# Row-tiled transposes, another order of the value products, and a selection product for the router's logits in a linear-attention kernel

## The chip, the cores and the metric

One core of a Trainium2 chip runs the whole program. The metric is the device time of one execution in microseconds (us). TensorE (PE; its weight loads are PEld), VectorE (DVE), ScalarE (ACT) and GpSimd (POOL) each run their own instructions in order and wait for each other by semaphores; SyncE (SP) issues most DMAs.

## The reference

Gated linear attention, then two expert layers. Only the attention is touched by the change.

```python
def _attn_ref(q, k, v, f_logit):        # B, H, S, D = 4, 8, 768, 48
    f = 1.0 / (1.0 + np.exp(-f_logit))
    for t in range(S):
        state = f[:, :, t, :, None] * state + np.einsum('bhd,bhe->bhde', k[:, :, t], v[:, :, t])
        y[:, :, t] = np.einsum('bhd,bhde->bhe', q[:, :, t], state)
# _moe_ref:  logits = x @ w_gate (3072 x 8); tokens go to 8 experts of 384 places each
#            in the order of their logits; relu(x @ w1[e]) @ w2[e]
# _moe2_ref: rms norm, then (silu(xn @ w_gate) * (xn @ w_val)) @ w_out
```

## The kernel before

The attention works on 16 units, each a batch and a pair of heads. Head 0 of a pair lies on partitions 0 to 47, head 1 on partitions 64 to 111; the 768 positions run along the free axis in six chunks of 128. In each chunk the keys are scaled by a scan of the decays (`W`, giving `kt`) and the queries by another (`P`, giving `qt`), so that a chunk is a masked product of `kt` and `qt` (`at`) times `v`, plus the state at the chunk's start (`st`) times `qt`.

The loop at the end of `attention` is a pipeline written out by hand. In turn `i` TensorE's queue holds, in this order: `values(i - 2)` (the outputs `yp`, from 10 products with `st` and 12 with `at`), `logits_turn` in three of the turns, `k_back(i)` (five chunks of `kt` transposed into `kn`), `inner(i)` (12 products into four banks, three chunks and one head to a bank), `sums(i)` (10 products into `U`), and `logits` in the turns in which a batch is complete. The router's logits of a batch leave `logits` as `lgT`, 4 pairs of heads with 32 rows each; the four are added up later: `logits_turn` transposes three blocks of 128 tokens into a bank, and `logits_sum` on VectorE reduces over the pairs into `lg`. The last batch goes through the same functions behind the loop's last values, and the routing starts on its `lg`.

VectorE's queue in turn `i` holds `scans(i + 1)` (scan `P`, reciprocal, scan `W`, then `logits_sum` if one is due, then `kt`) and then the scan `st` behind `sums(i)`. ScalarE copies out of PSUM: `YT` from `yp`, `kn`, `at`, `lgT`. GpSimd makes `qt` and masks `at`.

PSUM has eight banks: four in the pool behind `bank()`, taken in rotation by `k_back`, `inner`, `logits` and `logits_turn`, two for `yp`, one for `U`, and one for `one`, a column of ones that every scan reads as its second operand.

TensorE's instructions address a part of its array. `k_back` and `logits_turn` use all of it (128 rows, 128 columns), `inner` the two halves of the rows (64 by 128), `sums` and the products with `at` the two halves of the columns (128 by 64), the products with `st` quarters (64 by 64). One fp32 product of two heads stands in the trace as two passes for each head; a transpose is one pass.

Of the kernel before, what the change touches and what calls it, by code (L numbers as in the profile page):

```python
# [7 lines left out]
F32 = mybir.dt.float32  # L8
# [5 lines left out]
OP = mybir.AluOpType  # L14
AX = mybir.AxisListType
# [65 lines left out]
class Route:  # L81
# [27 lines left out]
    def range(self, n):  # L109

        nc, v = self.tc.nc, self.v
        m = self.m0[:, 0:n]
        nc.vector.tensor_reduce(out=m, in_=self.lg[:, 0:n], axis=AX.X, op=OP.max)
        nc.vector.tensor_reduce(out=v[:, 1:2], in_=self.lg[:, 0:n].rearrange("p n e -> p (n e)"), axis=AX.X, op=OP.min)
        nc.vector.tensor_reduce(out=v[:, 0:1], in_=m, axis=AX.X, op=OP.max)
        nc.vector.tensor_reduce(out=v[:, 2:3], in_=m, axis=AX.X, op=OP.min)
        nc.vector.tensor_scalar(v[:, 1:3], v[:, 1:3], -1.0, None, op0=OP.mult)
        self.n = n
# [149 lines left out]
def spin(nc, o, ident, n):  # L268

    for _ in range(n):  # L270
        nc.tensor.matmul(o, ident, ident, start=True, stop=True)
# [52 lines left out]
def attention(tc, fT, kT, qT, vL, YT, w_gate, lg, pmin, ident, gcol, rms_g, extra):  # L324
# [4 lines left out]
    nc = tc.nc  # L329
    NU, _, S = fT.shape  # L330
    B, H, D = 4, 8, 48
    C = 128
    NP = H // 2
    NC = S // C
    ctx = ExitStack()
    pool = lambda name, bufs, **kw: ctx.enter_context(tc.tile_pool(name=name, bufs=bufs, **kw))
    cst = pool("a_cst", 1)
    wk = pool("a_wk", 2)
    ps = pool("a_ps", 4, space=PSUM)
    psl = pool("a_psl", 1, space=PSUM)  # L340
# [7 lines left out]
    def raw(nm, i):  # L348
        return RAW[nm, i % NR]

    def load(names, i):
        if not 0 <= i < NU:
            return
        for nm in names:
            if nm == "v":
                nc.sync.dma_start(V[i % NV].rearrange("p n h d -> p (n h d)"), vL[i])
                continue
            src, t = dict(f=fT, k=kT, q=qT)[nm][i], raw(nm, i)
            if i < NR:
                nc.sync.dma_start(t, src)  # L360
                continue
            for h in range(2):
                nc.sync.dma_start(t[64 * h:64 * h + D], src[64 * h:64 * h + D])

    HF = (slice(0, S // 2), slice(S // 2, S))
    for t in HF:
# [5 lines left out]
    nc.gpsimd.memset(mask, 1.0)  # L372
    nc.gpsimd.affine_select(out=mask, in_=mask, pattern=[[1, C]], compare_op=OP.is_ge, fill=0.0, base=0,
                            channel_multiplier=-1)
    one = psl.tile([128, 1], F32, name="one")
    nc.vector.memset(one, 1.0)
    one = one[:, 0:1].to_broadcast([128, S])
    wgp = cst.tile([128, NP, 32], F32, name="wgp")
    nc.vector.memset(wgp, 0.0)
    YP = [psl.tile([128, 384], F32, name=f"yp{i}") for i in range(2)]  # L380
# [9 lines left out]
    def bank():  # L390
        return ps.tile([128, 384], F32, name="bank")

    G, FS, P, W, KT, QT, KN, AT, ST, LG, EZ = ({} for _ in range(11))

    def decays(i):
        if not 0 <= i < NU:
            return
        G[i] = wk.tile([128, S + 1], F32, name="G")
        FS[i] = wk.tile([128, NC], F32, name="fs")
        for t in HF if i == 0 else (slice(0, S),):  # L400
            nc.scalar.activation(G[i][:, t], raw("f", i)[:, t], AF.Sigmoid)
        nc.scalar.activation(FS[i], raw("f", i)[:, 0:S:C], AF.Sigmoid)
# [18 lines left out]
    def scans(i):  # L421
        g = G[i]
        P[i] = wk.tile([128, S], F32, name="P")
        W[i] = wk.tile([128, S], F32, name="W")
        nc.vector.memset(g[:, 0:S:C], BIG * 1.0e8)
        nc.vector.tensor_tensor_scan(out=P[i], data0=g[:, :S], data1=one, initial=1.0, op0=OP.mult, op1=OP.min)
        ends = P[i][:, C - 1:S:C]
        nc.vector.reciprocal(g[:, C:S + 1:C], ends)
        nc.vector.tensor_tensor_scan(out=W[i][:, ::-1], data0=g[:, S:0:-1], data1=one, initial=1.0, op0=OP.mult,
                                     op1=OP.max)  # L430
        while turned:
            logits_sum(*turned.pop(0))
        QT[i] = wk.tile([128, S], F32, name="qt", bufs=3)
        for g in range(2):
            t = slice(g * 384, g * 384 + 384)
            nc.gpsimd.tensor_tensor(out=QT[i][:, t], in0=raw("q", i)[:, t], in1=P[i][:, t], op=OP.mult)
        EZ[i] = wk.tile([128, NC - 1], F32, name="e")
        nc.gpsimd.tensor_tensor(out=EZ[i], in0=ends[:, 0:NC - 1], in1=FS[i][:, 1:], op=OP.mult)
        KT[i] = wk.tile([128, S], F32, name="kt")
        nc.vector.tensor_tensor(out=KT[i], in0=raw("k", i), in1=W[i], op=OP.mult)  # L440

    def ends(i):
        if on(i):
            nc.scalar.copy(pall[:, i], P[i][:, C - 1:S:C])
            nc.scalar.copy(Z[i % 2][:, :, 1:], EZ[i][:, None, :].to_broadcast([128, D, NC - 1]))

    def k_back(i, gs=(0, 1)):
        if 0 in gs:
            KN[i] = wk.tile([128, NC, 128], F32, name="kn")
        for g in gs:  # L450
            m = 3 - g
            o = bank().rearrange("p (n c) -> p n c", n=3)
            for n in range(m):
                c0 = (3 * g + n) * C
                nc.tensor.transpose(o[:, n, :], KT[i][:, c0:c0 + C], ident)
            nc.scalar.copy(KN[i][:, 3 * g:3 * g + m], o[:, 0:m])

    def inner(i, gs=(0, 1)):

# [29 lines left out]
    def values(i):  # L489

        b, p = units[i]
        yp = YL if i == NU - 1 else YP
        todo = [(h, n, True) for h, n in ((0, 1), (1, 3), (0, 2), (1, 4), (1, 5), (1, 1), (0, 3), (1, 2), (0, 4), (0, 5))]
        todo += [(h, n, False) for n in range(NC) for h in range(2)]
        first, last = {}, {}
        for m, (h, n, _) in enumerate(todo):
            first.setdefault((h, n // 3), m)
            last[h, n // 3] = m
        for m, (h, n, state) in enumerate(todo):
            d, c = slice(64 * h, 64 * h + D), slice(n * C, (n + 1) * C)  # L500
            nc.tensor.matmul(yp[n // 3][d, (n % 3) * C:(n % 3 + 1) * C],
                             ST[i][d, :, n] if state else V[i % NV][:, n, h, :],
                             QT[i][d, c] if state else AT[i][:, h, n, :],
                             start=m == first[h, n // 3], stop=m == last[h, n // 3])
        for g in range(2):
            cp = nc.vector.tensor_copy if g and i == NU - 1 else nc.scalar.copy
            cp(YT[0:112, b, p, 384 * g:384 * g + 384], yp[g][0:112])
# [8 lines left out]
        nc.scalar.copy(LG[b, g], o)  # L516

    def logits_turn(b, g):
        o = bank()
        for n in range(3):  # L520
            nc.tensor.transpose(o[:, n * 128:n * 128 + 128], LG[b, g][:, n * 128:n * 128 + 128], ident)
        turned.append((b, g, o))

    def logits_sum(b, g, o):
        nc.vector.tensor_reduce(out=lg[:, NC * b + 3 * g:NC * b + 3 * g + 3, :],
                                in_=o.rearrange("p (n a e) -> p n e a", n=3, a=NP)[:, :, 0:8], axis=AX.X, op=OP.add)

    YL = []
    on = lambda i: 0 <= i < NU
    turned = []  # L530
    o = bank()[:, 0:128]
# [10 lines left out]
    for i in range(-1, NU + 2):  # L542
        if i - 1 in extra:
            extra[i - 1](bank()[:, 0:256])
        if on(i - 2):
            values(i - 2)
        if on(i - 3) and units[i - 3][1] == NP - 1:
            for g in range(2):
                logits_turn(units[i - 3][0], g)
        load("v", i + 2 if i > -1 else NU)  # L550
        if i < 0:
            decays(1)
        if i > 0 and on(i):
            k_back(i)
        if i == NU - 1:
            extra["range"]()
        if i < 0:
            for t in HF:
                scans_half(t)
            for g in range(2):  # L560
                k_back(0, (g,))
                inner(0, (g,))
            ends(0)
        elif on(i + 1):
            scans(i + 1)
        if on(i):
            if i:
                inner(i)
            decays(i + 2)
            sums(i)  # L570
            if i == 0:
                spin(nc, bank()[:, 0:128], ident, 11)
            ends(i + 1)
        if on(i - 2) and units[i - 2][1] == NP - 1:
            for g in range(2):
                logits(units[i - 2][0], g)
            if i == NU + 1:
                for g in range(2):
                    logits_turn(units[i - 2][0], g)
                    logits_sum(*turned.pop(0))  # L580
        if i == NU - 1:
            extra["edges"](bank())
        load("fkq", i + 4)
        if i == NU - 1:
            for _ in range(2):
                YL.append(bank())
                nc.vector.memset(YL[-1][32:64], 0.0)
        if i == NU:
            nc.vector.tensor_reduce(out=pmin, in_=pall.rearrange("p a b -> p (a b)"), axis=AX.X, op=OP.min)
# [664 lines left out]
```

## Time and profile before

| | us |
|---|---|
| median of 3 runs (lowest, highest) | 832.44 (831.95, 832.62) |
| the profiled execution's own time | 832.29 |
| its span, first to last instruction | 830.6 |
| busy in the span: PE, PEld | 805.3, 777.4 |
| busy in the span: DVE, ACT, POOL | 485.7, 391.3, 274.0 |

The attention ends at about 116 us of the span, the routing follows until about 150 us, and the rest is the two expert layers, in which TensorE is hardly ever idle. Busy times of matmuls are modelled at their ends, and matmuls overlap: what a block of TensorE work costs is best read from its start to the start of the next block.

### The profile page before, as it was taken

The numbers are of one execution on the slowest core, as the hardware profiler recorded it, in microseconds if no ns is written. First come the engines' busy times: TensorE is split into PE (matmuls) and PEld (weight loads), VectorE is DVE, ScalarE is ACT, GpSimd is POOL, SyncE is SP. The second block draws the span as 40 slices with busy tenths as digits, with TensorE's granted clock in tenths as the row PEclk, the third lists the DMA queues.
The fourth block names the chain that finished last, engine by engine and source line by source line (L and its number), as shares of the span: only waits on it lengthen the run. The fifth ranks groups of instructions, "written<-read, shape, count | busy, mean of one in ns | idle before, by whom it ended". The sixth has DMA issues, their size and how long they took to land.

```text
span 830.6 us, 16688 instructions
## 1 busy us (share of the span) xinstructions
PE 805.3 (97%) x6641; PEld 777.4 (94%) x6641; DVE 485.7 (58%) x875; ACT 391.3 (47%) x834; POOL 274.0 (33%) x327
## 2 busy tenths in 40 slices
PE   8999996999999999999999999999999999999996
PEld 7888875899999999999999999999999999999996
DVE  8988868579888988575444434334343434334332
ACT  5777644256645555476343343424343443434221
POOL 7877600367777777250202010110102010110100
PEclk9999997899999999999999999999999999999999
DMA  9997227586887788341000000000000000000000
GB/s 270 224 219 193 58 92 290 184 298 226 284 280 245 248 282 301 127 152 39 10 12 20 1 20 2 20 1 20 4 17 20 1 21 1 20 1 21 1 20 20
DMA packets 43829, 88.56 MB, mean 107 GB/s; under 512 B 5440, under 2 KB 23104, under 8 KB 43744
## 3 DMA queue, kind: packets, MB, share of 16 engines
q1 hardware_dynamic: 34672, 70.89, 27.6%
q0 software_dynamic: 3072, 9.44, 3.4%
q10 hardware_dynamic: 6000, 7.09, 2.4%
q8 instruction: 54, 0.88, 0.5%
q14 instruction: 31, 0.25, 0.1%
HBM read 70.89 MB, written 16.52 MB: 105 GB/s over the span
## 4 chain that ended last, share of the span: by engine, by line
PE 61%; issue 9%; DVE 8%; ACT 2%; DMA 1%; POOL 1%; ACTq 0%; DVEq 0%; POOLq 0%
PE o L624 5%; PE o L622 5%; PE o L623 5%; PE g L622 5%; PE g L624 5%; PE g L623 5%; PE v L624 5%; PE v L623 5%; PE v L622 5%; PE x L623 3%; PE x L624 2%; PE x L622 2%; DVE nb L1006 2%; DVE w L813 2%; PE h L623 2%
## 5 line engine op out<-in xcount | busy, mean ns | idle before, releaser
L1178 DVE TENSOR_TENSOR hf<-sg,v 128x256 f32<-128x256 f32 x144 | 60.0, 417 | 165.1 <-PE v L624 114.9
L944 POOL TENSOR_TENSOR xlo<-xn,xhi 128x256 fp32r<-128x256 f32 x36 | 29.5, 823 | 311.9 <-ACT xhi L943 311.9
L1181 ACT CAST hh<-hf 128x256 fp32r<-128x256 f32 x144 | 58.6, 407 | 132.9 <-DVE hf L1178 132.9
L624 PE MATMUL g<-xhi,w 128*128 128x256 f32 x432 | 119.3, 276 | 0.0
L623 PE MATMUL g<-xlo,w 128*128 128x256 f32 x432 | 119.3, 276 | 0.0
L624 PE MATMUL v<-xhi,w 128*128 128x256 f32 x432 | 119.2, 276 | 0.0
L622 PE MATMUL v<-xhi,w 128*128 128x256 f32 x432 | 119.2, 276 | 0.0
L623 PE MATMUL v<-xlo,w 128*128 128x256 f32 x432 | 119.2, 276 | 0.0
L622 PE MATMUL g<-xhi,w 128*128 128x256 f32 x432 | 119.2, 276 | 0.0
L1182 DVE TENSOR_TENSOR hl<-hf,hh 128x256 fp32r<-128x256 f32 x144 | 61.3, 426 | 68.1 <-ACT hh L1181 67.6
L624 PE MATMUL o<-w,hl 128*128 128x384 f32 x288 | 98.6, 342 | 0.0
L622 PE MATMUL o<-w,hh 128*128 128x384 f32 x288 | 97.5, 339 | 0.2 <-ACT hh L1181 0.2
L623 PE MATMUL o<-w,hh 128*128 128x384 f32 x288 | 97.1, 337 | 0.0
L1176 ACT ACTIVATE sg<-g 128x256 f32<-128x256 f32 x144 | 55.3, 384 | 87.8 <-PE g L624 87.3
L622 PEld LDWEIGHTS g<-xhi,w 128*128 128x128 f32 x432 | 81.1, 188 | 0.0
L624 PEld LDWEIGHTS g<-xhi,w 128*128 128x128 f32 x432 | 81.1, 188 | 0.0
L622 PEld LDWEIGHTS v<-xhi,w 128*128 128x128 f32 x432 | 81.1, 188 | 0.0
L624 PEld LDWEIGHTS v<-xhi,w 128*128 128x128 f32 x432 | 81.1, 188 | 0.0
L623 PEld LDWEIGHTS v<-xlo,w 128*128 128x128 f32 x432 | 81.1, 188 | 0.0
L623 PEld LDWEIGHTS g<-xlo,w 128*128 128x128 f32 x432 | 81.0, 188 | 0.0
L1009 POOL TENSOR_TENSOR nr<-nr,ne 128x384 f32<-128x384 f32 x36 | 61.6, 1711 | 42.8 <-ACT hh L1082 11.8
L623 PE MATMUL x<-hl,w 128*128 128x384 f32 x192 | 65.7, 342 | 3.5 <-DVE hl L1083 3.5
(237 smaller groups left out, 1893.8 us busy)
## 6 DMA issues: line engine op xcount, KB each, us to landing
wraw<-in_moe_w_dram SPq DMA_DIRECT2D x32, 768.0 KB, 7.8
v<-in_v_rows_dram SPq DMA_DIRECT2D x16, 288.0 KB, 5.1
x_dram<-xrows SPq DMA_DIRECT2D x24, 192.0 KB, 5.4
nraw<-in_moe_w_gate_dram SPq DMA_DIRECT2D x12, 384.0 KB, 4.9
nraw<-in_moe_w_val_dram SPq DMA_DIRECT2D x12, 384.0 KB, 4.4
nraw<-in_moe_w_out_dram SPq DMA_DIRECT2D x12, 384.0 KB, 4.3
raw_f<-in_f_logit_turned_dram SPq DMA_DIRECT2D x26, 144.0 KB, 5.4
raw_k<-in_k_turned_dram SPq DMA_DIRECT2D x26, 144.0 KB, 4.6
```

What stands on the lines that cost most here:

```text
L622: nc.tensor.matmul(out, lhs[0], rhs[0], start=first, stop=False)
L623: nc.tensor.matmul(out, lhs[0], rhs[1], start=False, stop=False)
L624: nc.tensor.matmul(out, lhs[1], rhs[0], start=False, stop=last)
L813: eng.tensor_tensor(out=lo, in0=raw, in1=hi.bitcast(F32), op=OP.subtract)
L944: eng.tensor_tensor(out=lo, in0=s, in1=hi.bitcast(F32), op=OP.subtract)
L1006: nc.vector.scalar_tensor_tensor(out=b, in0=hw, scalar=-0x40000000, in1=b, op0=OP.bitwise_and, op1=OP.bitwise_or)
L1009: nc.gpsimd.tensor_tensor(out=r, in0=r, in1=e2.bitcast(F32), op=OP.mult)
L1176: nc.scalar.activation(sg, pg, AF.Silu)
L1178: nc.vector.tensor_tensor(out=h, in0=sg, in1=pv, op=OP.mult)
L1181: nc.scalar.copy(hh, h)
L1182: nc.vector.tensor_tensor(out=hl, in0=h, in1=hh.bitcast(F32), op=OP.subtract)
```

## The change

Three things are rewritten. `k_back` transposes each chunk head by head, 48 rows at a time, all chunks of a head into one bank of its own, and copies each bank with one instruction. `values` issues the 12 products with `at` ahead of the 10 with `st`. `logits_turn` replaces each transpose by a product with a constant matrix `sel` (128 by 8, four stacked unit matrices), which adds up the pairs; its outputs go to 192 columns of a bank that also holds `one`, and `logits_sum` is one copy for a batch instead of two reductions.

```diff
-    one = psl.tile([128, 1], F32, name="one")
+    bank0 = psl.tile([128, 512], F32, name="bank0")
+    one = bank0[:, 0:1]
     nc.vector.memset(one, 1.0)
-    one = one[:, 0:1].to_broadcast([128, S])
+    one = one.to_broadcast([128, S])
+    lgp = bank0[:, 64:64 + lg.shape[1] * 8].rearrange("p (n e) -> p n e", e=8)
+    sel = cst.tile([128, 8], F32, name="sel")
+    nc.vector.tensor_reduce(out=sel, in_=ident.rearrange("q (p e) -> q e p", p=NP)[:, 0:8, :], axis=AX.X, op=OP.add)
...
     def k_back(i, gs=(0, 1)):
         if 0 in gs:
             KN[i] = wk.tile([128, NC, 128], F32, name="kn")
-        for g in gs:
-            m = 3 - g
-            o = bank().rearrange("p (n c) -> p n c", n=3)
-            for n in range(m):
-                c0 = (3 * g + n) * C
-                nc.tensor.transpose(o[:, n, :], KT[i][:, c0:c0 + C], ident)
-            nc.scalar.copy(KN[i][:, 3 * g:3 * g + m], o[:, 0:m])
+        a, m = (0, NC - 1) if len(gs) == 2 else (3 * gs[0], 3 - gs[0])
+        o = [bank()[:, 0:m * D].rearrange("p (n d) -> p n d", n=m) for _ in range(2)]
+        for n in range(m):
+            for h in range(2):
+                d = slice(64 * h, 64 * h + D)
+                nc.tensor.transpose(o[h][:, n, :], KT[i][d, (a + n) * C:(a + n + 1) * C], ident[d, d])
+        for h in range(2):
+            nc.scalar.copy(KN[i][:, a:a + m, 64 * h:64 * h + D], o[h])
...
     def values(i):
-        todo = [(h, n, True) for h, n in ((0, 1), (1, 3), (0, 2), (1, 4), (1, 5), (1, 1), (0, 3), (1, 2), (0, 4), (0, 5))]
-        todo += [(h, n, False) for n in range(NC) for h in range(2)]
+        todo = [(h, n, False) for n in range(NC) for h in range(2)]
+        todo += [(h, n, True) for h, n in ((0, 1), (1, 3), (0, 2), (1, 4), (1, 5), (1, 1), (0, 3), (1, 2), (0, 4), (0, 5))]
...
     def logits_turn(b, g):
-        o = bank()
         for n in range(3):
-            nc.tensor.transpose(o[:, n * 128:n * 128 + 128], LG[b, g][:, n * 128:n * 128 + 128], ident)
-        turned.append((b, g, o))
-
-    def logits_sum(b, g, o):
-        nc.vector.tensor_reduce(out=lg[:, NC * b + 3 * g:NC * b + 3 * g + 3, :],
-                                in_=o.rearrange("p (n a e) -> p n e a", n=3, a=NP)[:, :, 0:8], axis=AX.X, op=OP.add)
+            nc.tensor.matmul(lgp[:, NC * b + 3 * g + n, :], LG[b, g][:, n * 128:n * 128 + 128], sel, start=True, stop=True)
+        if g:
+            turned.append(slice(NC * b, NC * b + NC))
+
+    def logits_sum(t):
+        nc.vector.tensor_copy(lg[:, t], lgp[:, t])
```

TensorE's queue from the `sums` of the turn in which the first batch is complete to the `sums` of the next turn, before, with the output tile, the moving and the stationary operand and the shape of the output (L501 is `values`, L513 `logits`, L521 `logits_turn`):

```order
L482 MATMUL U<-v_113,kn 48x48 x10
L513 MATMUL bank<-YT,wgp 32x384 x8
L501 MATMUL yp_129<-qt,st 48x128
...
L501 MATMUL yp_130<-qt,st 48x128 x2
L501 MATMUL yp_129<-at,v_112 48x128 x6
L501 MATMUL yp_130<-at,v_112 48x128 x6
L521 MATMUL bank<-ident,lgT 128x128 x6
L455 MATMUL bank<-ident,kt 128x128 x5
L468 MATMUL bank<-qt,kt 128x128 x12
L482 MATMUL U<-v_114,kn 48x48 x10
```

The same place now:

```order
L487 MATMUL U<-v_113,kn 48x48 x10
L518 MATMUL bank<-YT,wgp 32x384 x8
L506 MATMUL yp_131<-at,v_112 48x128 x6
L506 MATMUL yp_132<-at,v_112 48x128 x6
L506 MATMUL yp_131<-qt,st 48x128
...
L506 MATMUL yp_132<-qt,st 48x128 x2
L525 MATMUL bank_125<-sel,lgT 128x8 x6
L459 MATMUL bank<-ident,kt 128x48 x10
L473 MATMUL bank<-qt,kt 128x128 x12
L487 MATMUL U<-v_114,kn 48x48 x10
```

The products with `at` moved ahead of those with `st`; in a turn without logits (no L513, no L521) they now follow `sums` of the turn before directly; `k_back` has ten transposes of 48 columns for five of 128; the six products with `sel` stand where six transposes (L521) stood.

VectorE's queue in that turn, with the semaphores each waits for, before:

```order
L426 SCALAR_TENSOR_TENSOR P<-G,one 128x768 [waits DVE_49,Pool_49]
L428 RECIPROCAL G<-P 128x6 [waits DVE_49]
L429 SCALAR_TENSOR_TENSOR W<-G,one 128x768 [waits DVE_49]
L525 TENSOR_REDUCE lg<-bank 128x24 [waits PE_49] x2
L440 TENSOR_TENSOR kt<-raw_k_107,W 128x768 [waits DMAHW6_49,DMAHW5_49,DVE_49]
```

And now:

```order
L430 SCALAR_TENSOR_TENSOR P<-G,bank_125 128x768 [waits DVE_49,PE_49,Pool_49]
L432 RECIPROCAL G<-P 128x6 [waits DVE_49]
L433 SCALAR_TENSOR_TENSOR W<-G,bank_125 128x768 [waits DVE_49]
L530 COPY lg<-bank_125 128x48
L444 TENSOR_TENSOR kt<-raw_k_107,W 128x768 [waits DMAHW6_49,DMAHW5_49,DVE_49]
```

The scan `P` of the next unit, which reads `one`, now waits for TensorE, that is for the products with `sel` into the same bank; the reductions' wait behind `W` is gone. In the other turns the scans' waits are as before.

## Rows read from the trace of the kernel before

**Rows 1.** The page, first part: busy us (share of the span) and instructions

```profile
PE 805.3 (97%) x6641; PEld 777.4 (94%) x6641; DVE 485.7 (58%) x875; ACT 391.3 (47%) x834; POOL 274.0 (33%) x327
```

**Rows 2.** Busy time by stretch: length, PE PEld DVE ACT POOL, granted clock, DMA

```profile
47.28:53.66 6.38, 5.69 (x95) 4.97 (x94) 4.54 (x7) 4.08 (x11) 3.30 (x7) 1.00 1.02 228
53.66:59.35 5.69, 5.69 (x95) 5.01 (x94) 5.43 (x7) 4.56 (x12) 4.73 (x7) 1.00 1.03 221
...
72.87:78.50 5.63, 5.63 (x95) 4.95 (x93) 3.63 (x7) 4.08 (x11) 2.40 (x6) 1.00 0.78 210
```

**Rows 3.** Timeline of VectorE: two neighbouring scans `P` (start, length)

```profile
27.75 1.75 DVE L426 TENSOR_TENSOR_SCAN P<-G,one 128x768 f32<-128x768 f32 x1
...
33.36 1.75 DVE L426 TENSOR_TENSOR_SCAN P<-G,one 128x768 f32<-128x768 f32 x1
```

**Rows 4.** Timeline of TensorE over one turn with logits and the next

```profile
65.04 0.77 PE L455 MATMUL bank<-ident,kt 128*128 128x128 f32 x5
65.73 1.68 PE L468 MATMUL bank<-qt,kt 48*128 48x128 f32 x24
67.35 0.66 PE L482 MATMUL U<-v,kn 128*48 128x48 f32 x20
67.93 1.50 PE L513 MATMUL bank<-YT,wgp 112*32 112x384 f32 x16
69.36 1.42 PE L501 MATMUL yp<-qt,st 48*48 48x128 f32 x20
70.71 1.52 PE L501 MATMUL yp<-at,v 128*48 128x128 f32 x24
72.16 0.88 PE L521 MATMUL bank<-ident,lgT 128*128 128x128 f32 x6
72.87 0.71 PE L455 MATMUL bank<-ident,kt 128*128 128x128 f32 x5
73.51 0.38 PE L468 MATMUL bank<-qt,kt 48*128 48x128 f32 x2
```

**Rows 5.** Timeline of ScalarE around 65 us

```profile
64.50 0.48 ACT L507 COPY YT<-yp 112x384 f32<-112x384 f32 x1 [0.64 <-PE yp L501]
65.16 0.48 ACT L507 COPY YT<-yp 112x384 f32<-112x384 f32 x1 [0.18 <-PE yp L501]
65.68 0.75 ACT L456 COPY kn<-bank 128x384 f32<-128x384 f32 x2
```

**Rows 6.** Timeline of weight loads: two neighbouring ones of fp32 products, of transposes

```profile
119.26 0.19 PEld L195 LDWEIGHTS T<-far,ident 128*128 128x128 f32 x1
...
119.37 0.19 PEld L195 LDWEIGHTS T<-far,ident 128*128 128x128 f32 x1
...
72.16 0.14 PEld L521 LDWEIGHTS bank<-ident,lgT 128*128 128x128 f32 x1 [0.18 <-ACT YT L507]
...
72.21 0.14 PEld L521 LDWEIGHTS bank<-ident,lgT 128*128 128x128 f32 x1
```

**Rows 7.** Timeline of TensorE in the first turn with transposed logits

```profile
48.67 0.34 PE L468 MATMUL bank<-qt,kt 48*128 48x128 f32 x1 [0.69 <-POOL e L438]
```

**Rows 8.** Timeline of VectorE in that turn

```profile
44.61 1.75 DVE L426 TENSOR_TENSOR_SCAN P<-G,one 128x768 f32<-128x768 f32 x1
...
48.30 0.40 DVE L525 TENSOR_REDUCE lg<-bank 128x24 f32<-128x96 f32 x2
48.61 0.95 DVE L440 TENSOR_TENSOR kt<-raw_k,W 128x768 f32<-128x768 f32 x1
```

**Rows 9.** Timeline of the attention's end, TensorE and VectorE

```profile
109.93 1.73 PE L501 MATMUL bank<-qt,st 48*48 48x128 f32 x20 [0.35 <-DVE bank L587]
...
114.54 1.23 PE L521 MATMUL bank<-ident,lgT 128*128 128x128 f32 x6
...
113.15 0.56 DVE L507 COPY YT<-bank 112x384 f32<-112x384 f32 x1 [2.87 <-PE bank L501]
...
115.81 0.26 DVE L525 TENSOR_REDUCE lg<-bank 128x24 f32<-128x96 f32 x1 [0.42 <-PE bank L521]
```

More of the change, by code (lines that the diff above doesn't have):

```diff
@@ L431, in scans @@
         while turned:
-            logits_sum(*turned.pop(0))
+            logits_sum(turned.pop(0))
         QT[i] = wk.tile([128, S], F32, name="qt", bufs=3)
@@ L579, in attention @@
                     logits_turn(units[i - 2][0], g)
-                    logits_sum(*turned.pop(0))
+                logits_sum(turned.pop(0))
         if i == NU - 1:
```

## The prediction

> **What bounds the kernel now.** I began with the page: TensorE is busy for 97% of the span and no other engine for more than 58% [rows 1]. That share is an average, so the stage of the change was read next, stretch by stretch. [...] A turn without logits is 5.69 long; the one exception is the turn at 47.28, 5.69 busy in 6.38 [rows 2]. So TensorE's queue bounds the attention, and what leaves that queue leaves the time, unless someone else is close behind. VectorE is: where nothing holds it up, its scans `P` start 5.61 apart [rows 3], 0.08 less than TensorE needs. The attention is about 100 of 830 us, and the routing behind it starts on its last logits, so I count a microsecond of it as one of the kernel.
>
> The timeline of TensorE prices the blocks, from each start to the next [rows 4]: `k_back` 0.69, `inner` 1.62, `sums` 0.58, `logits` 1.43, the `st` products 1.35, the `at` products 1.45, `logits_turn` 0.71. Without the logits that is 5.69 again.
>
> **The price of changing the array's shape.** Behind the six transposes of `logits_turn`, which use the same part of the array, the five of `k_back` last 0.64 (72.87 to 73.51) instead of 0.69, and the six themselves, with no change of shape behind them, 0.71. Two unknowns and a step: 6 steps + start = 0.71, 5 steps + end = 0.64, 5 steps + start + end = 0.69. That gives 0.11 for a transpose, 0.05 for the start after a change of shape and 0.09 for the end before one [rows 4]. The 12 steps of the `at` block (1.32 of 1.45) leave 0.13 for the two, which agrees.
>
> **Term 1: `at` ahead of `st`.** `sums` and the `at` products both use 128 by 64, so where `at` follows `sums` one change of shape is gone: 0.14. Before, a turn had five changes; `at` to `st` and `st` to `k_back` replace `st` to `at` and `at` to `k_back`, price for price. Of the 14 intervals between `k_back` of unit 1 and of unit 15, three have `logits` between `sums` and the values and one a single full-array transpose; ten gain. Ten times 0.14 is **-1.4** (bounds: 0, if the array does not take the two for one shape, and -2.0 if all 14 gain).
>
> **Term 2: `k_back`.** `k_back` (64 by 128 now) and `inner` have one shape, so one more change goes, another 0.14. Ten transposes of 48 columns in place of five of 128 cost about the same or less if the heads run side by side, as those of `inner` do: its 24 passes take 12 steps in 1.62 [rows 4]. But there is a loop through ScalarE. `inner`'s second half writes the two banks that `k_back` has just filled, and must wait for the `kn` copies. Before, the last `kn` copy ended at 65.68 + 0.75 = 66.43, that is 1.39 after `k_back`'s start [rows 5], and `sums` began 0.92 later [rows 4]; 12 steps and a change of shape account for only some 1.46 of `inner`'s 1.62, so it was waiting for that copy already. Now the copies of both `yp` banks come late: with `st` last, both banks are complete only at the end of the values, where before the first was copied at 64.50, well ahead of the second at 65.16 [rows 5]. So ScalarE does two `YT` copies (0.37 apart, half of the 0.75 for two copies of like size), then a `kn` copy of 240 columns (0.25 to the next, by columns) and another (0.36): from 0.04 to 0.12 after `k_back`'s start (the last `YT` copy before began 0.12 after it) this ends at 1.39 to 1.47. `sums` then starts 2.31 to 2.39 after `k_back`, where it started 2.31 after. In 11 turns I take +0.03; in the three with `sel`, in which the `YT` copies are long done and only the `kn` copies count (0.61 for 0.75), about -0.08. Together **+0.1**. The gain of `k_back` is eaten by ScalarE. Bounds: if the copies do not gate, -0.14, or -0.30 with `inner`'s old wait of 0.16 gone too (-2.0 to -4.2 in 14 turns); +0.09 in 11 (+1.0) at the other end.
>
> **Term 3: the products with `sel`.** Six fp32 products are 12 passes, each with a load of 128 columns. Two such loads start 0.11 apart (119.26, 119.37), those of transposes 0.05 to 0.06 (72.16, 72.21) [rows 6]. With only eight moving columns the load sets the step: 12 times 0.11, a start and an end, 1.46. Before, `logits_turn` cost 0.71 less the 0.05 that it saved `k_back`. So +0.8 in each of three turns, **+2.4**; the lower bound, with the transposes' load price of 0.06, is +0.2 a turn (+0.6), the upper, with the eight columns (0.007 a pass) not hidden, 0.9. I take the price of the fp32 loads, since these are fp32 products.
>
> **Term 4: the bank.** In the first turn with transposed logits, `inner` began at 48.67 [rows 7], 1.39 after `k_back` at 47.28, not 0.64. The view names GpSimd, but `inner` takes the bank of `logits_turn`, and VectorE freed that in the reductions at 48.30 to 48.70 [rows 8]. The new `logits_turn` takes no bank of the pool: **-0.75**.
>
> **Term 5: the attention's end.** It is serial. The values of the last unit begin at 109.93, after VectorE's memset of their second bank; with `at` first, that bank is wanted only 0.65 later, and the `st` block's 1.73 [rows 9] becomes the 1.42 of the others [rows 4]: -0.3. Then `YT`'s first half is complete only with `st`'s end, and `logits` starts some 0.2 later than it could; its second half, which waited for VectorE's copy of 113.15 to 113.71 [rows 9], comes 0.1 later on balance. The transposes at 114.54 become twelve load-bound passes, 0.64 for each half instead of 0.33; the second reduction (115.81, 0.26) becomes one copy of 48 columns, 0.1 to 0.2. Sum: the first `lg` reader starts **+0.3** later (bounds 0 and +0.5).
>
> **The wait of scan `P`.** In the turns with `sel`, `P` of the next unit waits for the products, in a bank shared with `one`. Before, it ran at 44.61 [rows 8], 2.7 ahead of `k_back` at 47.28 [rows 2]. Queued behind it are `W`, `kt` and `st`, and GpSimd's `qt`. Now it starts with `k_back`; from `P` to the end of `kt` is 48.61 + 0.95 - 44.61 = 4.95 [rows 8]. TensorE asks for that `kt` 5.6 after `k_back`'s start (5.63 at 72.87 [rows 2]), so 0.6 is spare, and in the two turns that follow VectorE needs 5.61 to TensorE's 5.55: the spare stays above 0.4. I price it at nothing; its cover is gone once `P` starts 0.6 later than that. [...]
>
> **Sum.** -1.4 + 0.1 + 2.4 - 0.75 + 0.3 = +0.65. `sel`'s one reduction stands in VectorE's first microseconds, in which it idles. The profiled execution took 832.29, inside the three runs; 832.29 + 0.65 = **832.9**, 0.05% above the median. A measurement of this kernel can tell about 0.2%, 1.7 us.
>
> **Rivals.**
> *No change that can be measured* (the forecast): 0.67.
> *ScalarE does not gate, faster*: if the `kn` copies end early enough, term 2 is -2.0 to -4.2, in the middle -3.1, and the sum -2.55: 829.7; with the cheap loads of term 3 as well, 827.9. For it: ScalarE idles 0.64 before a `YT` copy [rows 5]. Against it: `inner` waited for that copy before. 0.17.
> *The loads of `k_back` run one after another, slower*: ten loads at 0.11 put the last transpose 1.1 after the first instead of 0.5, the second `kn` copy ends at 1.75, and each `k_back` to `sums` takes 2.66 for 2.31: 14 times 0.35, 4.9, in place of term 2, 837.7. It decides as soon as a pair of transposes takes more than 0.15. [...] Against it: transposes load at 0.05 to 0.06 [rows 6], ten of which are 0.6, and `inner`'s pairs overlap [rows 4]. 0.08.
> *The scan's wait reaches TensorE, slower*: if `P` starts 1.6 after `k_back` rather than with it, 1.0 is lost in each of three turns, 3.0 on top of the sum: 835.9. For it: VectorE is only 0.08 faster than TensorE. It decides from 0.6. 0.08.
>
> **Numbers.** Faster 0.17, within 0.2% 0.67, slower 0.16. The range runs from 829.7 (the first rival alone) to 835.9 (the last), and leaves out the serial loads and part of the first rival; the forecast's own range is 831.3 to 834.1.
>
> **What would show it.** Right: `sums` directly followed by `at` 0.09 sooner and the `at` block at 1.40; `k_back` shorter than 0.69, yet `sums` still 2.3 to 2.4 after it, with the last `kn` copy ending 1.4 after; `logits_turn` at 1.4 to 1.5; `inner` 0.4 to 0.6 after `k_back` in the turn near 47 us; VectorE idle for about 3 ahead of `P` in three turns, until TensorE has done its part, without TensorE waiting for `kt`. Wrong: a turn below 5.5 (ScalarE does not gate, and VectorE's 5.61 is not a bound either, since it gains on the turns with logits), a turn above 5.8, or idle time of TensorE ahead of `k_back`.

## The result: slower, and most of it behind the part that was changed

The changed kernel takes 840.4 us (median of 4 runs, 838.34 to 841.52) against 832.2 (831.38 to 832.62) for the kernel before. The ratio is 1.0087, with a 95% interval of 1.0069 to 1.0104 (the two medians alone give 1.0099). The forecast was 832.9 with a range to 835.9, so the prediction was wrong, by 7.5 us. The profiled execution took 841.52, its span is 839.8.

The attention was read first. The timeline of TensorE over a turn without logits, in the changed kernel (start, length, line, tiles, count):

```profile
59.71 0.51 PE L459 MATMUL bank<-ident,kt 48*128 48x48 f32 x10
60.05 2.04 PE L473 MATMUL bank<-qt,kt 48*128 48x128 f32 x24
62.02 0.65 PE L487 MATMUL U<-v,kn 128*48 128x48 f32 x20
62.51 1.48 PE L506 MATMUL yp<-at,v 128*48 128x128 f32 x24
63.92 1.42 PE L506 MATMUL yp<-qt,st 48*48 48x128 f32 x20
65.27 0.51 PE L459 MATMUL bank<-ident,kt 48*128 48x48 f32 x10
```

From `k_back` to `k_back` it is 5.56; the forecast gives 5.58 (5.69 - 0.14 + 0.03). `k_back` is down to 0.34, and `sums` still starts 2.31 behind it. ScalarE's timeline of that turn says why:

```profile
59.73 0.86 ACT L512 COPY YT<-yp 112x384 f32<-112x384 f32 x2 [1.28 <-PE yp L506]
60.47 0.63 ACT L461 COPY kn<-bank 128x240 f32<-128x240 f32 x2
```

The last `kn` copy ends at 61.10, 1.39 behind `k_back`: two `YT` copies now stand ahead of it, as counted. The turn behind the products with `sel` is another matter:

```profile
45.76 1.50 PE L525 MATMUL bank<-sel,lgT 128*128 128x8 f32 x12
47.19 0.51 PE L459 MATMUL bank<-ident,kt 48*128 48x48 f32 x10
47.54 2.57 PE L473 MATMUL bank<-qt,kt 48*128 48x128 f32 x24
50.05 1.04 PE L487 MATMUL U<-v,kn 128*48 128x48 f32 x20
50.88 1.98 PE L506 MATMUL yp<-at,v 128*48 128x128 f32 x24
52.79 1.42 PE L506 MATMUL yp<-qt,st 48*48 48x128 f32 x20
```

The block with `sel` takes 1.43 (1.46 forecast) and `inner` starts 0.35 behind `k_back`, so the wait for the bank [rows 7] is gone. But `inner` takes 2.51 for 1.97, `sums` 0.83 for 0.49 and `at` 1.91 for 1.41. TensorE is busy for the whole turn, so this is no wait; the view by stretches names the cause (length, busy PE PEld DVE ACT POOL, granted clock, DMA):

```profile
47.19:54.14 6.95, 6.95 (x99) 6.36 (x98) 6.61 (x8) 3.57 (x10) 4.73 (x7) 0.75 0.61 150
54.14:59.71 5.57, 5.54 (x101) 4.92 (x100) 5.36 (x7) 4.22 (x12) 4.72 (x7) 1.00 0.90 213
73.83:80.80 6.97, 6.97 (x100) 6.35 (x100) 6.63 (x8) 3.56 (x10) 4.73 (x7) 0.76 0.35 98
100.49:105.88 5.39, 5.39 (x101) 4.92 (x100) 5.16 (x6) 2.73 (x8) 3.39 (x5) 1.00 0.01 3
```

In two of the three turns behind `sel` the mean granted clock is 0.75 and 0.76: in the first of them it reads 1.00 until 48, 0.75 from 48 to 49, 0.50 until 51, 0.55 until 52 and 1.00 from there, taken in single microseconds, which makes some 3.4 us at 0.50. The third turn, without a fall, takes 5.39. So each of the two falls costs 1.57 (6.95 and 6.97 for 5.39). In the rows of [rows 2] the clock is 1.00 throughout.

The two falls, 3.1 together, are more than the attention's whole delay (2.5), since other terms came out lower. The milestones (starts in a timeline; for `idx` the end of its last write) show where the rest is:

| | before | after | later by |
|---|---|---|---|
| first routing product (L217) | 118.47 | 120.94 | 2.47 |
| `idx` (rows of the tokens) written, end of the routing | 146.73 | 149.47 | 2.74 |
| first transposes of gathered rows (`x`) | 151.74 | 156.87 | 5.13 |
| end of the span | 830.6 | 839.8 | 9.2 |

Some 70% (6.5 of 9.2) arise behind `idx`, in code that the diff does not touch. The timeline there, of before and then of the changed kernel (GpSimd issues the gathers of `xrow`; in brackets the idle time ahead and what ended it):

```profile
146.56 0.17 DVE L321 CAST idx<-t 128x8 int32<-128x8 f32 x1
147.68 1.23 POOL L836 DMA_INDIRECT xrow<-x_dram,idx  x1 [6.69 <-DVE idx L321]
151.74 0.52 PE L1102 MATMUL x<-ident,xrow 128*128 128x128 f32 x3 [0.56 <-PEq L876]
```

```profile
149.30 0.17 DVE L321 CAST idx<-t 128x8 int32<-128x8 f32 x1
152.72 1.23 POOL L840 DMA_INDIRECT xrow<-x_dram,idx  x1 [8.99 <-SPq L880]
156.87 0.52 PE L1106 MATMUL x<-ident,xrow 128*128 128x128 f32 x3 [4.30 <-DMA xrow<-x_dram,idx]
160.79 0.41 PE L626 MATMUL h<-xhi,w 128*128 128x256 f32 x1
161.00 0.41 PE L627 MATMUL h<-xlo,w 128*128 128x256 f32 x1
```

The first gather starts 3.25 behind the end of `idx` where it started 0.95 behind; the releaser named is SyncE's branch, and nothing that the gather reads ends there. TensorE idles 4.30, and soon after it starts again its clock falls: from 160 to 164 it is at 0.50, the products with `w` start 0.21 apart, and the stretches read

```profile
156.87:164.00 7.13, 6.13 (x29) 5.37 (x30) 1.09 (x3) 0.92 (x3) 2.33 (x4) 0.56 0.66 215
164.00:168.00 4.00, 3.17 (x23) 2.70 (x23) 2.59 (x3) 0.97 (x2) 1.16 (x4) 0.93 0.17 49
168.00:172.00 4.00, 4.00 (x16) 4.00 (x15) 4.00 (x5) 2.34 (x3) 0.00 (x0) 0.58 0.71 243
```

Before, every stretch of 4 us from 152 to 180 is at 1.00. So the loss is 2.7 up to `idx`, 2.4 until the first `x`, and 4.1 in what follows it.

### The profile page after: what moved, and what is told of

Read it like the earlier page. It is cut to its first block, busy times and chain, and to the rows that moved or that the text cites. A ratio compares the mean times of both kernels' runs of the same rounds, so it can differ in the third digit from the quotient of the medians.

```text
span 839.8 us, 16899 instructions
## 1 busy us (share of the span) xinstructions
PE 811.4 (97%) x6745; PEld 784.1 (93%) x6745; DVE 482.8 (57%) x872; ACT 387.3 (46%) x836; POOL 276.6 (33%) x327
## 4 chain that ended last, share of the span: by engine, by line
PE 63%; issue 8%; DVE 7%; ACT 2%; DMA 1%; POOL 1%; ACTq 0%; DVEq 0%; POOLq 0%
PE o L628 5%; PE o L626 5%; PE o L627 5%; PE g L626 5%; PE g L627 5%; PE g L628 5%; PE v L628 5%; PE v L626 5%; PE v L627 5%; PE x L627 3%; PE x L628 3%; PE h L627 3%; PE h L626 3%; PE x L626 3%; PE h L628 3%
## 5 line engine op out<-in xcount | busy, mean ns | idle before, releaser
L626 PE MATMUL h<-xhi,w 128*128 128x384 f32 (+2 forms) x198 | 68.9, 348 | 0.7 <-ACT xhi L1118 0.6
```

What stands on the lines that cost most here:

```text
L626: nc.tensor.matmul(out, lhs[0], rhs[0], start=first, stop=False)
```

## The experiments

In all twelve runs two things were read from the trace (one execution of each run): the granted clock of the three turns behind `logits_turn`, and the start of the first gather behind the end of `idx` ("behind `idx`" from here on, rounded from the trace's own times, which the rows shown give to 0.01). The kernel before ran beside each set: its median was 832.07 us with runs 1 to 4, 832.73 with runs 5 to 8, and 831.92 (one execution) with runs 9 to 12. Ratios are against that. The diffs are against the changed kernel, or the kernel before in run 6; `...` stands for further lines of a diff.

**1. Without `sel`.** `k_back` and `values` as changed; transposes, reductions and `one` as before.

```diff
...
-            nc.tensor.matmul(lgp[:, NC * b + 3 * g + n, :], LG[b, g][:, n * 128:n * 128 + 128], sel, start=True, stop=True)
+            nc.tensor.transpose(o[:, n * 128:n * 128 + 128], LG[b, g][:, n * 128:n * 128 + 128], ident)
...
```

> The changed kernel with the transposes and reductions of before in place of the products with sel (the bank is not shared). [...] Rival 'the other two edits cost it' (the row-tiled transposes let the clock fall): low clock in turns of the attention again, 838 to 840. Rival 'the expert stage's start goes by chance of position': 831 or 837, with the gather more than 2 us behind idx in the second case.

831.79 us, ratio 0.9991 (0.9975 to 1.0006). All turns are at 1.00 (5.38 behind `logits_turn`, 5.56 the others), and the gather is 0.96 behind `idx`:

```profile
47.77:53.15 5.38, 5.38 (x100) 4.92 (x100) 3.55 (x7) 3.53 (x11) 4.12 (x7) 1.00 1.03 245
72.21:77.59 5.38, 5.38 (x100) 4.93 (x100) 3.54 (x7) 3.53 (x11) 4.13 (x7) 1.00 0.89 216
```

The other two edits cost nothing. The trace shows their gain in the attention (below, at terms 1 and 2); in the time of the kernel it is too small to be measured.

**2. `sel` alone.** The kernel before, with the diff's `bank0`, `lgp`, `sel`, `logits_turn` and `logits_sum`.

> The kernel before with only the products with sel and the shared bank. Theory 'clock': the two low-clock turns are there as in the changed kernel, and the attention ends some 4 later than before (2.5 + the 1.4 that the order of the value products gave): 840 to 842. Rival 'it takes the narrow transposes behind the products too': clock 1.00 throughout the attention, end of attention +1.7 (2.4 - 0.75), 833 to 835.

837.09 us, 1.0057 (1.0035 to 1.0079). The rival is right on the clock and missed the time. No turn falls below 1.00:

```profile
47.24:52.91 5.67, 5.67 (x95) 5.00 (x94) 5.36 (x7) 4.17 (x11) 3.59 (x5) 1.00 0.86 202
72.78:78.44 5.66, 5.66 (x95) 4.99 (x94) 5.36 (x7) 4.18 (x11) 3.59 (x5) 1.00 0.46 108
98.30:103.97 5.67, 5.67 (x96) 4.99 (x95) 5.36 (x7) 3.35 (x9) 3.60 (x5) 1.00 0.01 3
```

So behind the five full transposes the 8 columns did not bring the clock down. And yet 5.0 us are lost, with the first routing product at 118.87, only 0.40 later than before, and the gather 3.16 behind `idx`.

**3. `sel` 64 columns wide.**

```diff
...
-    sel = cst.tile([128, 8], F32, name="sel")
...
+    sel = cst.tile([128, 64], F32, name="sel")
+    for e in range(0, 64, 8):
+        nc.vector.tensor_reduce(out=sel[:, e:e + 8], in_=ident.rearrange("q (p e) -> q e p", p=NP)[:, 0:8, :], axis=AX.X, op=OP.add)
...
```

> The changed kernel with sel 64 columns wide (8 copies side by side), so that each product moves 64 columns and not 8; weight loads, waits and the shared bank stay, and the outputs of each batch take the same columns. Theory 'clock, from the 8 columns': the block still takes about 1.45 (load-bound) but no turn falls below 1.00; attention ends 2.8 sooner than in the changed kernel, 832 to 834. Rival 'scan P's wait for TensorE costs it': nothing changes, two turns of 6.95, 840.

The turns behind `sel`:

```profile
47.94:53.32 5.38, 5.38 (x99) 4.91 (x99) 5.15 (x6) 3.56 (x10) 3.38 (x5) 1.00 0.53 122
73.06:78.44 5.38, 5.38 (x99) 4.91 (x99) 5.15 (x6) 3.56 (x10) 3.38 (x5) 1.00 0.47 111
98.18:103.56 5.38, 5.38 (x99) 4.91 (x98) 5.15 (x6) 2.73 (x8) 3.38 (x5) 1.00 0.01 3
```

The block still takes 1.49, scan `P` still waits for it, and no turn falls. With these transposes behind it, then, the 8 columns decide, and the scan's wait costs nothing. The time is 838.35, 1.0072 (1.0053 to 1.0091), not the 832 to 834 expected: the gather is 3.27 behind `idx` here too.

**4. `sel` in a bank of the pool**, `one` in its own, so that `P` waits for no product.

```diff
...
-            nc.tensor.matmul(lgp[:, NC * b + 3 * g + n, :], LG[b, g][:, n * 128:n * 128 + 128], sel, start=True, stop=True)
+            nc.tensor.matmul(LP[b][:, 3 * g + n, :], LG[b, g][:, n * 128:n * 128 + 128], sel, start=True, stop=True)
...
```

> The changed kernel with the products with sel in a bank of the pool, taken in rotation, and one in a bank of its own: scan P no longer waits for them, TensorE's products are the same. Theory 'clock': two low-clock turns of about 6.95 as in the changed kernel, perhaps longer by the wait for the bank, 839 to 841. Rival 'scan P's wait': VectorE does not idle ahead of P, all turns 5.6, 831 to 833.

838.21 us, 1.0077 (1.0053 to 1.0101). Two of the three turns fall to 0.77 and take 7.36 and 7.37 (0.21 of it a wait for a `kn` copy):

```profile
73.80:81.16 7.36, 7.15 (x100) 6.38 (x100) 4.19 (x7) 3.59 (x10) 3.53 (x6) 0.77 0.53 122
100.84:108.21 7.37, 7.16 (x99) 6.38 (x99) 2.87 (x8) 2.77 (x8) 3.50 (x6) 0.77 0.01 2
```

Scan `P` waits for nothing here and the clock falls all the same, so the rival is out. In the profile the end of the attention is later than in the changed kernel (first routing product at 123.74), but the gather is on time:

```profile
151.73 0.16 DVE L321 CAST idx<-t 128x8 int32<-128x8 f32 x1
152.85 1.23 POOL L841 DMA_INDIRECT xrow<-x_dram,idx  x1 [6.69 <-DVE idx L321]
```

It starts 0.96 behind `idx`, and the span is 835.5. (The six executions of this run spread from 836.60 to 841.68; only the one of 837.22 has a trace.) So a late routing does not delay the gather; what the late ones have in common, up to here, is the shared bank.

What has GpSimd to do with that bank? Its queue of waits shows it. Where the scan `P` has waited for TensorE, GpSimd's `qt` behind it need not. Such a row, before and in the changed kernel:

```
L436 TENSOR_TENSOR qt<-raw_q_110,P 128x384 [waits DMAHW0_49,DMAHW7_49,DVE_49,PE_49]
L440 TENSOR_TENSOR qt<-raw_q_110,P 128x384 [waits DMAHW7_49,DMAHW0_49,DVE_49]
```

There are three such rows, and each has one separate semaphore instruction fewer ahead of it (in the traces GpSimd has 52 of them ahead of the first gather before, and 49 now). So 196 instead of 199 GpSimd instructions stand ahead of the first gather in the shared-bank kernels (the changed one, runs 2 and 3), and 199 in the others so far (before, runs 1 and 4). Runs 5 and 6 move that number and leave the attention as it is.

**5. Three GpSimd memsets more in the changed kernel.**

```diff
+    pad = cst.tile([1, 3], F32, name="pad")
+    for c in range(3):
+        nc.gpsimd.memset(pad[:, c:c + 1], 0.0)
```

> The changed kernel with three GpSimd memsets of one element more, early, so that the first gather stands at the same number in GpSimd's program as before (199 instructions ahead of it, not 196). Theory 'position' (the shared bank takes three waits for TensorE out of GpSimd's program, and the gather, three places earlier, starts 3.26 behind idx and not 0.96): the gather starts about 0.96 behind idx, TensorE idles about 0.6 ahead of it, the expert stage starts at 1.00, and the end lies about 684 behind idx instead of 690: 834 to 835, the rest being the attention's 2.7. Rival 'clock alone' (the attention's low-clock turns are the cause, the gather's place is not): 840 as before.

835.65 us, 1.0038 (1.0020 to 1.0055). The gather (DVE's `idx`, GpSimd, TensorE):

```profile
150.64 0.17 DVE L324 CAST idx<-t 128x8 int32<-128x8 f32 x1
151.76 1.23 POOL L843 DMA_INDIRECT xrow<-x_dram,idx  x1 [6.67 <-DVE idx L324]
155.85 0.52 PE L1109 MATMUL x<-ident,xrow 128*128 128x128 f32 x3 [1.62 <-PEq L883]
```

The gather starts 0.95 behind `idx` again, and the products with `w` run at 1.00, with two falls in the attention as in the changed kernel.

**6. Three fewer in the kernel before**, by moving early memsets to VectorE.

```diff
-    nc.gpsimd.memset(up0, -(2.0 ** -7))
+    nc.vector.memset(up0, -(2.0 ** -7))
-        nc.gpsimd.memset(lim[:, c:c + 1], a)
-        nc.gpsimd.memset(lim[0:1, c:c + 1], b)
+        eng = nc.gpsimd if c else nc.vector
+        eng.memset(lim[:, c:c + 1], a)
+        eng.memset(lim[0:1, c:c + 1], b)
```

> The kernel before with three early GpSimd memsets moved to VectorE, so that its first gather has 196 instructions ahead of it as in the changed kernel; nothing else. Theory 'position': the gather starts 3.2 behind idx, TensorE idles over 2 ahead of the expert stage and its clock falls there; idx is where it was, the end 4.4 to 6.5 later, 836.5 to 838.5. Rival 'something else in the changed kernel delays the gather' (its later routing, the shared bank): 832, no change.

836.8 us, 1.0046 (1.0030 to 1.0062):

```profile
147.14 0.17 DVE L322 CAST idx<-t 128x8 int32<-128x8 f32 x1
150.45 1.23 POOL L837 DMA_INDIRECT xrow<-x_dram,idx  x1 [8.90 <-issue]
155.46 0.88 PE L1103 MATMUL x<-ident,xrow 128*128 128x128 f32 x3 [4.26 <-DMA xrow<-x_dram,idx]
```

The gather is 3.15 behind `idx`, with neither a shared bank nor `sel`. Three tiny instructions moved out of an idle engine's queue cost 4 us. The stretch 155.46 to 160.60 is at 0.50.

**7. More idle products ahead of the late gather** (32 for 12 in `slots`).

> The changed kernel with 32 idle products instead of 12 at the end of the routing, so that TensorE is busy until the late gather arrives. Theory 'cold start' (of the 6.4 lost behind idx 2.3 are the gather's, and some 4 the low clock that follows TensorE's idle 4.3): the first xrow transposes are where they were, the products with w behind them run at 1.00, 836 to 837. [...]

847.52 us, 1.0172 (1.0154 to 1.0189), far above the 836 to 837 of the theory.

```profile
150.56 9.22 PE L271 MATMUL spin<-ident 128*128 128x128 f32 x64
162.60 0.30 PE L1106 MATMUL x<-ident,xrow 128*128 128x128 f32 x1 [2.82 <-PEq L880]
165.25 0.69 PE L1106 MATMUL x<-ident,xrow 128*128 128x128 f32 x2 [2.35 <-issue]
```

The idle products ended at 159.78, and TensorE starts again only 2.82 later, behind its own branch (`PEq`, the `If` on `flag`). Then 2.35 more of idle time stand ahead of the second transpose. So the idle products put the branch off and did not fill the gap: TensorE idles twice, and from 165.25 to 168.00 the clock is at 0.50. What the two idle stretches wait for is not shown. Whether a TensorE that stays busy keeps its clock at 1.00 is not told by this run.

**8. Both repairs**: wide `sel` and three memsets.

> Both repairs: sel 64 columns wide and the three GpSimd memsets. Theory 'clock and position together': no low clock in the attention (end of attention as in the run with the wide sel alone, 0.2 behind before), the gather 0.96 behind idx: 832 to 833, which is the forecast of the prediction. Rival: a part is still missing, 835 or more.

832.70 us, 0.9999 (0.9987 to 1.0012): all turns are at 1.00, and the gather is 0.95 behind `idx`:

```profile
148.06 0.17 DVE L324 CAST idx<-t 128x8 int32<-128x8 f32 x1
149.18 1.23 POOL L844 DMA_INDIRECT xrow<-x_dram,idx  x1 [6.70 <-DVE idx L324]
```

With both causes away the kernel takes as long as the one before, and what the prediction gave it. One thing does not fit: in the profiled execution (834.81, the second slowest of twelve) the 4 us behind the first `x` are at 0.57, though the gather is on time; TensorE idles 2.13 ahead of them, behind its own branch.

**9 to 12. How wide is the bad place?** The changed kernel with one, two and nineteen memsets of run 5, and with five early ones moved to VectorE (one execution each). In what was expected of them, 0.96, 1.7, 2.5 and 3.2 are the gather's start behind `idx`, in us.

> The changed kernel with one early GpSimd memset more (197 instructions ahead of the first gather). [...] Rival 'each instruction counts': about 2.5.

> Two memsets more (198 ahead). Theory 'a place in the program': 3.2 or 0.96, and with the run with one memset this names the place to one instruction. Rival 'each instruction counts': about 1.7.

> Nineteen memsets more (215 ahead). Theory 'a place in the program': far behind the place as the kernel before is, 0.96 behind idx. Rival 'any odd place': a third value.

> The changed kernel with five early GpSimd memsets moved to VectorE (191 ahead). [...] Rival 'only the changed kernel's own place is bad': 0.96 and nothing else late, 834 to 836.

| instructions ahead of the gather | 191 | 196 | 197 | 198 | 199 | 215 |
|---|---|---|---|---|---|---|
| gather behind `idx`, us | 0.96 | 3.15 to 3.32 | 3.09 | 0.96 | 0.95 to 0.96 | 0.96 |
| turns with a fall, of three | 2 | 2 | 2 | 1 | 2 | 2 |
| time, us | 835.46 | 840.4 | 839.63 | 836.48 | 835.65 | 837.52 |

The falls and the times are those of the changed kernel (196) and of runs 5 (199) and 9 to 12; the gathers are those of all kernels with that number. A time from one execution tells no difference of 2 us (before spread from 830.84 to 835.03 in the set of run 5), so the gather is what counts here. It has two values only, and a place of at least two and at most six instructions: it is late neither before it nor behind it, so the rival of run 12 holds. The DMA view shows a difference that goes with it. From 0.6 to 1.3 us behind `idx`, in the changed kernel and in run 6, there is one packet of the kind `instruction`:

```profile
q14 instruction: 1, 0.01, 4.4%
```

```profile
q14 instruction: 1, 0.01, 4.0%
```

In the same stretch of before and of run 5 no such packet is there, and the gather starts in it. That the gather waits for this packet is not shown: the view does not say which engine a packet is for, and this one has landed (at 151.05 in the changed kernel) 1.7 us before the gather starts. At the bad place the late start took 2.1 to 2.4 us of the path (3.1 to 3.3 for 0.96); its cause is not shown.

## Why the prediction was wrong, point by point

- **What bounds it.** Right for the attention: cut at the starts of `k_back` of units 1 to 15, TensorE is busy for the whole of 13 of the 14 turns of before (5.69 of 6.38 in the one at 47.28), at a granted clock of 1.00. What was missing: "the routing behind it starts on its last logits, so I count a microsecond of it as one of the kernel". The step from the routing to the first gather has a delay of its own, 0.95 to 3.32 behind `idx`, which goes by the gather's place in GpSimd's program, and that one counted most.
- **Term 1** (-1.4) and **term 2** (+0.1): right, in size and in mechanism. The seven plain intervals are at 5.56 to 5.57, `at` at 1.41, `sums` 2.31 behind `k_back`, the last `kn` copy at 1.39. Behind a logits turn without a fall the turn is 5.39 where 5.63 or 5.64 stood; -0.14 and -0.08 give 5.41. The start of the attention shifts by up to 2 us between traces, so its length is best counted from `k_back` of unit 1 to the first `rows` product: 99.71 before, 98.77 in run 6 (the same attention, without the wait of term 4), 97.55 in run 1, 99.41 in runs 3 and 8, 102.38 in the changed kernel. Run 1 against run 6 is -1.2, where the two terms give -1.3.
- **Term 3** (+2.4): the block is right (1.43); in the turns with it, +0.73 each (8.56 for 7.83), 2.2 together. But the term prices only the block itself and takes the turns behind it to stay at a clock of 1.00. **This is the first step that failed.** The runs show falls of the clock in one or two of the three turns behind the block, at 1.57 each, 3.1 in the profile of the changed kernel. No rival had the clock in it.
- **Term 4** (-0.75): the wait is gone, but it was no steady cost. In run 6, whose attention is that of before, the turn is at 5.63 and not 6.38, though it still takes the bank:

```profile
48.25:53.88 5.63, 5.63 (x95) 4.95 (x93) 3.63 (x7) 4.08 (x11) 2.39 (x6) 1.00 0.96 232
```

- **Term 5** (+0.3): right for what it names, the first `lg` reader, which starts 13.15 behind `k_back` of the last unit where it started 12.75 behind. But TensorE does not wait for it at once: its first `rows` product is at 12.72, before 12.77, and its first routing product at 15.06, before 15.12. At `idx` 0.27 of it may be left (2.74 later for 2.47).
- **Scan `P`** priced at nothing: right. VectorE idles 3.37 ahead of it (4.34 and 4.36 in the other two turns) and TensorE never waits; nor does it in run 3, whose turns behind the block are the short ones of 5.38:

```profile
47.36 1.75 DVE L430 TENSOR_TENSOR_SCAN P<-G,bank 128x768 f32<-128x768 f32 x1 [3.37 <-PE bank L525]
```

- **The second step that failed** is the price of the shared bank: I followed its wait to VectorE and TensorE, and not the three waits that it takes away from GpSimd. They move the gather in the program, which costs 2.3 us directly. In all it costs 4.1 to 6.3, by medians, each less that of before in its set: run 6 is 4.1 above before; the changed kernel is 8.2 above and run 5, with the gather moved back, 2.9; run 3 is 6.3 above and run 8 is level with it. The prediction's own scan wait, priced at nothing, was no cost; what the same edit did to GpSimd's queue was in no term and no rival.
- **Sum.** Run 8 has every term of the forecast without the two effects and measures 832.7 for 832.9. That near is in part luck: a difference under some 1 us cannot be told, and term 4 (-0.75) depended on a wait that the trace of before has and that of run 6 has not. The clock in the attention is worth some 3 us (run 5 against run 8: 835.65 and 832.70), the place of the gather the rest.

What stays open: why the fall comes in some of the turns and not in all; what the late gather waits for; and how the 4.1 behind the late `x` divide between the low clock and the later gathers that follow (the sixth starts 15.6 behind `idx` in the changed kernel, 10.2 before). Run 7 was to part them and did not. All six late traces have a low clock in the first 4 us behind the first `x` or soon after, but so have two with an early gather (run 8 as said, and run 11, where 164 to 168 is at 0.60, the first `x` being at 156.14). No run beats the kernel before by more than can be measured; run 1 is the nearest.

## What to carry to other kernels

Here a block of products with 8 columns cost its own time (1.43 us), and in two of the three turns behind it the granted clock fell (a mean of 0.75 and 0.76), at 1.57 us each: look at the clock in the stretch behind a narrow block, not at the block alone. When a change adds or removes waits, follow them to every engine: three waits fewer in GpSimd's program left 196 instructions ahead of the first gather instead of 199, and it started 3.25 us behind its last wait for 0.95. To tell such an accident from the change's own cost, shift the program by a few small instructions, as runs 5 and 6 do, and measure again.

## What the runs showed of the hardware

- **The clock falls in a TensorE that hardly idles.** Eight kernels (the changed one and runs 4, 5, 7 and 9 to 12) have the 8-column products followed by the ten transposes of 48 columns: in 15 of their 24 turns behind them the clock falls, in the first one shown to 0.50 for some 3.4 us (a mean of 0.75 over 6.95). TensorE is busy for all but 0.04 of the turn that ends with the products and for the whole turn behind it, but for 0.21 in run 4. With full transposes behind (run 2), with 64 columns (runs 3 and 8) or with transposes in place of the products (run 1, before and run 6), none of 18. So neither alone brought it down here. The evidence for each alone is thin, three turns in one trace of run 1 and of run 2: at 15 in 24, three in a row without a fall would come by chance about once in 20 (an estimate from these counts). The six turns of runs 3 and 8 leave little room for that.
- **A position in the program can cost 4 us.** With 196 or 197 GpSimd instructions ahead of the gather it starts 3.1 to 3.3 us behind the end of its last wait; with 191, 198, 199 or 215 it starts 0.96 behind. Run 6 (196, nothing else changed in the attention) is 4.1 us slower than before.
- **A branch can stand in the path too.** Behind the idle products of run 7 TensorE started again 2.82 us later, with its own branch (`PEq`) named as what ended the wait; before, 0.56 later. What the 2.82 went into is not shown.
